# Early pairs loaded four tokens to a partition, softmax sums inverted from seven numbers, weight sides stored contiguously, and a planner with other durations

## The chip, the cores and the metric

The kernel runs on one core of a Trainium2 chip. The metric is the device time of one execution in microseconds. Besides the run times there is one profiled execution, whose trace gives every instruction of TensorE (PE; its weight loads are PEld), VectorE (DVE), ScalarE (ACT), GpSimd (POOL) and of the DMA queues (SP's, and a few on ACT and POOL).

## The reference

Attention with normalised queries and keys, then a gated feed-forward block, all in fp32 from fp64 weights:

```python
q, k, v: (8, 12, 448, 64)          # batch, heads, tokens, head size
q_n = q / sqrt(mean(q*q) + 1e-6) * g_q ;  k_n likewise
attn = softmax(q_n @ k_n.T / 8) @ v
x = attn.transpose(0, 2, 1, 3).reshape(3584, 768)
out = (silu(x @ w_gate) * (x @ w_val)) @ w_out     # 768 -> 1536 -> 768
```

The softmax needs, for each head and query, the sum of the exponentials over all keys, and the division by it.

## The kernel before, in words

**Units of work.** A *pair* is two heads of one batch; there are 48. Two batches make one *block* of the feed-forward part, so there are four blocks of twelve pairs. Pairs 0 to 11 are *early*: they run before the first block's products. The twelve pairs of a later block run beside the down products of the block before it. The matrix products are done with fifteen products of 3 x 3 sub-blocks; their left and right operands are sums and differences of sub-blocks, called *sides*. The weight sides are made once by `convert` (24 tiles: load of raw fp64 words, two ACT passes L1218 and L1222, three DVE steps for each half L1240, L1246, L1252, twelve POOL sums L1271 and L1274), stored to DRAM (`up_sides`, `down_sides`, L1299) and loaded for every block by `load_sides` (L1360) into one of two `ws` buffers.

**A pair.** `load` brings q and k. Two pairs are *natural*, four tokens to a partition (L732, one DMA a tile); the others come as 32 x 32 pieces, four DMAs a tile (L737). ACT squares them (L767), DVE sums the squares (L787 or L793), and for the pairs that are not natural the two halves of the head are exchanged by four ACT copies (L803) and added (L807). ACT and DVE form the inverse root (L682 to L690), POOL scales (L827 or L834). The operands are turned by DVE (L865; the queries then scaled on ACT, L868), or for natural pairs by PE (L853) with a drain on DVE (L859) and one on ACT (L861). Then come scores (L912), exponentials (L927), the products with v (L988), and the sums of exponentials over the keys by a product with a constant (L1019). For early pairs this last product takes all four chunks of exponentials; for the others POOL and DVE add the chunks first (L932, L938).

**The division.** The sums stand as 224 columns, repeated over 32 partitions each. DVE takes their reciprocal (L1054). For early pairs PE spreads it over the partitions by a product with the matrix `chosen` (L1062); for the others ACT does so with eight copies of 32 x 224 (L1072). ACT copies one half of the weighted sums (L1077), DVE adds the other (L1080) and multiplies (L1084).

**The feed-forward part.** `block` makes 120 up products (L1400, two matmuls each, gate and value in turn, in two banks each), whose results ACT copies (L1342) or DVE combines (L1344, L1346, L1348), then 30 down products of four matmuls each (L1574), which the next pairs' attention is laid between.

**What sets the order.** Nothing is scheduled at run time. Each piece of work is given to `Order.add` with its engine, a planned duration, a due time `when`, a rank and what it follows; `Order.run` then fills each engine's queue by the earliest planned start, ties going to the earlier due time. So the durations and the modelled DMA times fix every engine's queue, and each engine keeps to its queue in order.

```python
if piece["kb"]:
    self.dma = max(self.dma, end) + piece["kb"] / 300.0
    end = self.dma + 1.8
```

Of the kernel before, what the change touches and what calls it, by code (L numbers as in the profile page):

```python
# [359 lines left out]

class Order:
# [10 lines left out]
    SWITCH = dict(PE=0.17, ACT=1.3)  # L372

    def __init__(self, pools, begin):
        self.begin = begin
        self.pools = {name: [None] * n for name, n in pools.items()}
        self.turn = dict.fromkeys(pools, 0)
        self.users = {}
        self.pieces = []
        self.free = {}  # L380
        self.port = 0.0
        self.dma = 0.0
        self.last = {}
        self.mode = {}

    def add(
        self, engine, us, when, emit, after=(), takes=(), uses=(), port=False, kb=0, group=None,
        mode=None, early=None, rank=0.0, slack=0.1,
    ):
        piece = dict(  # L390
            engine=engine, us=us, when=when, emit=emit, takes=takes, port=port, kb=kb,
            group=group, mode=mode, early=early, rank=rank, slack=slack,
# [10 lines left out]
    def start(self, piece):  # L403
# [6 lines left out]
        for before in piece["after"]:  # L410
            if before["end"] is None:
                return None
            at = max(at, before["end"] + piece["slack"] * (before["engine"] != piece["engine"]))
        for name, _ in piece["takes"]:
            old = self.pools[name][self.turn[name] % len(self.pools[name])]
            for user in self.users.get(old, ()):
                if user["end"] is None:
                    return None
                at = max(at, user["end"] + 0.1)
        return at  # L420

    def run(self, lookahead=400):
# [3 lines left out]
        while any(left.values()):  # L426
            best = None
            for engine, pieces in left.items():
# [15 lines left out]

                late = 0.7 if engine == "POOL" else 0.0
                if choice and (
                    best is None
                    or choice[0] + late < best[0] - 0.3
                    or choice[0] + late < best[0] + 0.3
                    and self.key(choice[1]) < self.key(best[1])  # L450
                ):
                    best = (choice[0] + late, choice[1])
# [8 lines left out]
            if piece["mode"] and self.mode.get(piece["engine"]) != piece["mode"]:  # L461
                end += self.SWITCH[piece["engine"]]
                self.mode[piece["engine"]] = piece["mode"]
                if piece["mode"] in self.begin:
                    self.begin[piece["mode"]]()
            self.last[piece["engine"]] = piece
# [3 lines left out]
            if piece["kb"]:  # L470
                self.dma = max(self.dma, end) + piece["kb"] / 300.0
                end = self.dma + 1.8
# [5 lines left out]
def fast(  # L478
# [60 lines left out]
    NATURAL = (0, 1)  # L539
# [9 lines left out]
        qk=4, v=2, t=2, QT=2, KT=2, e=4, ea=7, eh=2, sums=1, inv=1, rd=1, rows=3, st=2, at=2, ss=2,  # L549
# [15 lines left out]
    OFTEN = dict(w1=0, w2=1, w3=2, w4=3, rows=4, inv=7)  # L565
# [49 lines left out]
    up_sides = [dram.tile([P, 15, 2, NC2, P], F32, name=f"up_sides{g}") for g in range(NG)]  # L615
    down_sides = dram.tile([P, 15, 2, NG, P], F32, name="down_sides")
# [13 lines left out]
    chosen = const.tile([P, 2, P], F32, name="chosen")  # L630
# [42 lines left out]
    SPREAD = 6.0  # L673

    def inverse_root(m, sums, of, when, rank=0.0):
# [9 lines left out]
        def improve():  # L685
# [7 lines left out]
            "ACT", 0.5, when, estimate, after=[sums], uses=[("ss", m)], takes=[("rr", m)],  # L693
# [3 lines left out]
            "DVE", 0.45, when + 1.0, improve, after=[first], uses=[("ss", m), ("rr", m)],  # L697
# [9 lines left out]
    def attention(m):  # L707
# [19 lines left out]
        def load(x, src):  # L727
            def emit():
# [11 lines left out]
            both = m == 0 and src is k  # L740
            queue = nc.scalar if both else nc.sync
            return add(
                "ACT" if both else "SP", 0.5 if natural else 1.4 if both else 2.4, ready - 28.0, emit, takes=[("qk", (m, x))], kb=224, early=25.0,
# [15 lines left out]
        load_v = add("SP", 2.4, ready - 16.0, load_values, takes=[("v", m)], kb=256, early=25.0)  # L759

        def square(x):
# [6 lines left out]
            if m == 0 and x:  # L768
                for _ in range(4):
                    nc.tensor.matmul(banks[0], chosen[0:R, 0], of, start=True, stop=True)  # L770

        squares = []
        for x in range(2):
            squares.append(
                add(
                    "ACT", 0.53, ready - 18.0, lambda x=x: square(x),
# [28 lines left out]
        def both():  # L805
# [6 lines left out]
            "DVE", 1.1, ready - 17.0, summed, after=squares, uses=[("t", m)], takes=[("ss", m)]  # L812
        )
        if not natural:
            sums = add("ACT", 0.9, ready - 16.0, swap, after=[sums], uses=[("ss", m)])
            sums = add("DVE", 0.15, ready - 15.0, both, after=[sums], uses=[("ss", m)])
# [6 lines left out]
        def scale(x):  # L823
            if natural:
# [16 lines left out]
                "POOL", 1.0, ready - 9.0, lambda x=x: scale(x), after=[rr], port=True,  # L841
# [32 lines left out]
        if natural:  # L874
            of_turned = ("st", (m, "turned"))
            kt, qt = [
                add(
                    "PE", 0.8, ready - 6.0, lambda x=x: turn(x), after=[scaled[1 - x]],
                    uses=[("t", m)] + [of_turned] * (1 - x), takes=[of_turned] * x, mode="full",
                )  # L880
                for x in (1, 0)
            ]
            kt = add(
                "DVE", 0.64, ready - 5.0, lambda: drain(1), after=[kt], takes=[("KT", m)],
# [3 lines left out]
                "ACT", 0.6, ready - 5.0, lambda: drain(0), after=[qt, gains], takes=[("QT", m)],  # L888
# [3 lines left out]
            "DVE", 0.62, ready - 6.0, lambda: transpose(1), after=scaled[:1], takes=[("KT", m)],  # L892
# [3 lines left out]
            "DVE", 0.62, ready - 6.0, lambda: transpose(0), after=scaled[1:],  # L896
# [3 lines left out]
            "ACT", 0.65, ready - 5.0, queries, after=[qt, gains], uses=[("qk", (m, 0))],  # L900
# [42 lines left out]
        for j in (3, 0, 1, 2):  # L943
# [4 lines left out]
                "PE", 0.41 if half else 0.76, when, lambda j=j: scores(j),  # L948
# [5 lines left out]
                "ACT", 0.5 if half else 0.92, when + 1.0, lambda j=j: exps(j),  # L954
# [3 lines left out]
            if j in (1, 2) and not early:  # L958

                def more_sums(j=j):  # L960
                    if j == 1:
# [5 lines left out]
                        "POOL", 2.15, when + 2.0, more_sums, after=[ex[j], ex[0], *adds[-1:]],  # L967
# [62 lines left out]
        for j in range(NJ):  # L1030
            half = j == NJ - 1
            last = add(
                "PE", 0.41 if half else 0.76, when + 0.01 * j, lambda j=j: weighted(j),
# [737 lines left out]
```

## Time and profile before

| | us |
|---|---|
| median of 3 runs | 1483.65 (1482.71 to 1483.81) |
| the profiled execution, its own time | 1484.42 |
| its span, first to last instruction | 1482.6 |
| first up product starts | 139.92 |
| first up products of blocks 1, 2 and 3 start | 503.9, 854.2, 1204.4 |
| last down product ends | about 1475.3 |

The page's first part gives the busy time of each engine and the number of instructions. The forty slices show the same over time, a digit being tenths of a slice. In a row of stages come the limits of the stage, its length, then busy time and number of instructions for PE, PEld, DVE, ACT and POOL, the granted TensorE clock, the busy share of the DMA engines and their GB/s. In the timeline a row is start, length, engine, line, operation, output and input, and in brackets how long the engine had stood idle and what released it. SPq and ACTq are the instructions that issue DMAs.

### The profile page before, as it was taken

What the parts mean: (1) busy time and instruction counts of PE and PEld (TensorE: products, weight loads), DVE (VectorE), ACT (ScalarE), POOL (GpSimd) and SP (SyncE); (2) the same over time, 40 slices, a digit from 0 to 9 for tenths busy, and PEclk for the clock granted to TensorE, in tenths of its full rate; (3) what the DMA queues carried; (4) which work ended last, traced back from release to release, by engine and by line L of the source; (5) the groups of instructions that cost most, each with busy time, mean ns of one, the idle gap of its engine ahead of it and who ended that gap; (6) DMA issues with size and microseconds to landing.
All of it is one profiled execution on the core that took longest, in us unless ns stands there. A gap on an engine that the chain in (4) does not pass through costs nothing.

```text
span 1482.6 us, 19482 instructions
## 1 busy us (share of the span) xinstructions
PE 1435.1 (97%) x6696; PEld 680.7 (46%) x6696; DVE 914.8 (62%) x1403; ACT 680.7 (46%) x1358; POOL 416.0 (28%) x470
## 2 busy tenths in 40 slices
PE   6989999999999999999999999999999999999998
PEld 2434554443444455544444445554444445555553
DVE  3878897877978544355886733454786753432533
ACT  5864544437775321445767422354676532122100
POOL 3545585636444100012534200011343410000000
PEclk8999999999999999999999999999999999999999
DMA  6677999974453431533344432352444442222235
GB/s 166 160 162 215 294 331 335 289 213 92 98 117 84 111 107 71 144 98 89 78 110 107 101 118 72 110 132 77 97 101 103 89 123 85 80 98 73 83 98 107
DMA packets 409457, 193.30 MB, mean 130 GB/s; under 512 B 316804, under 2 KB 391428, under 8 KB 403204
## 3 DMA queue, kind: packets, MB, share of 16 engines
q1 hardware_dynamic: 397840, 190.35, 47.8%
q10 hardware_dynamic: 11380, 1.61, 0.7%
q8 instruction: 55, 0.90, 0.3%
q14 instruction: 54, 0.44, 0.1%
q0 software_dynamic: 128, 0.00, 0.0%
HBM read 157.29 MB, written 34.60 MB: 129 GB/s over the span
## 4 chain that ended last, share of the span: by engine, by line
PE 73%; ACT 3%; DVE 3%; issue 1%; DMA 1%; SPq 1%; ACTq 0%; DVEq 0%
PE mm L1574 22%; PE mm L1400 20%; PE at L1400 20%; PE st L912 6%; PE at L988 5%; PE st L1019 1%; ACT spare L1072 1%; ACT es L927 1%; SPq L737 1%; DVE rd L1054 1%; DVE ss L807 0%; DMA work<-in_k_dram 0%; DMA out_dram<-spare 0%; DVE ss L793 0%; ACT ss L803 0%
## 5 line engine op out<-in xcount | busy, mean ns | idle before, releaser
L1400 PE MATMUL at<-xs,ws 128*128 128x448 f32 x960 | 400.6, 540 | 4.3 <-DVE v L1346 3.1
L1400 PE MATMUL mm<-xs,ws 128*128 128x448 f32 x960 | 401.0, 540 | 3.6 <-DVE spare L1348 2.2
L1400 PEld LDWEIGHTS at<-xs,ws 128*128 128x128 f32 x960 | 181.9, 190 | 184.8 <-issue 172.1
L1400 PEld LDWEIGHTS mm<-xs,ws 128*128 128x128 f32 x960 | 181.6, 190 | 184.3 <-issue 172.0
L834 POOL TENSOR_TENSOR work<-work,rr 128x448 f32<-128x448 f32 x92 | 101.8, 1126 | 480.1 <-DVE rr L690 353.3
L1574 PE MATMUL mm<-gt,ws 128*128 128x448 f32 x448 | 177.2, 545 | 0.0
L912 PE MATMUL st<-work 64*64 64x448 f32 (+1 forms) x1536 | 156.4, 514 | 18.0 <-ACT es L927 7.5
L1344 DVE TENSOR_TENSOR gt<-gt,mm 128x448 f32<-128x448 f32 x64 | 39.7, 620 | 184.2 <-PE mm L1400 181.9
L1574 PE MATMUL mm<-hs,ws 128*128 128x448 f32 x384 | 152.1, 545 | 0.9 <-DVE ss L688 0.9
L927 ACT ACTIVATE es<-st 128x896 f32<-128x896 f32 x129 | 114.1, 912 | 54.3 <-PE at L988 42.6
L932 POOL TENSOR_TENSOR sums<-es 128x896 f32<-128x896 f32 x36 | 75.8, 2104 | 196.0 <-PE st L1019 83.4
L1474 ACT ACTIVATE st<-gt 128x448 f32<-128x448 f32 x96 | 52.3, 546 | 168.9 <-DVE gt L1348 90.3
L1072 ACT COPY spare<-rd 32x224 f32<-32x224 f32 x288 | 108.1, 375 | 35.4 <-DVE rd L1054 31.1
L1574 PEld LDWEIGHTS mm<-gt,ws 128*128 128x128 f32 x448 | 82.9, 190 | 84.2 <-issue 80.6
L988 PE MATMUL at<-es,v 64*64 64x448 f32 x1032 | 109.9, 544 | 2.7 <-DVE ss L688 2.5
L1342 ACT COPY gt<-mm 128x448 f32<-128x448 f32 x80 | 42.5, 532 | 140.4 <-PE mm L1400 140.4
L1574 PEld LDWEIGHTS mm<-hs,ws 128*128 128x128 f32 x384 | 71.1, 190 | 72.9 <-issue 70.6
L912 PEld LDWEIGHTS st<-work 64*64 64x64 f32 x1536 | 50.8, 135 | 98.8 <-issue 38.1
L1342 ACT COPY v<-at 128x448 f32<-128x448 f32 x96 | 51.1, 532 | 85.1 <-PE at L1400 81.0
L932 POOL TENSOR_TENSOR sums<-sums,es 128x896 f32<-128x896 f32 x36 | 78.7, 2186 | 2.8
L865 DVE STREAM_TRANSPOSE work<-work 128x448 f32<-128x448 f32 x92 | 56.6, 627 | 25.5 <-POOL work L834 22.8
L988 PEld LDWEIGHTS at<-es,v 64*64 64x64 f32 x1032 | 39.5, 134 | 63.0 <-issue 58.7
(161 smaller groups left out, 1589.1 us busy)
## 6 DMA issues: line engine op xcount, KB each, us to landing
ws<-up_sides SPq DMA_DIRECT2D x32, 1024.0 KB, 5.0
ws<-down_sides SPq DMA_DIRECT2D x16, 1024.0 KB, 5.0
ws<-down_sides SPq DMA_DIRECT2D x28, 512.0 KB, 4.3
ws<-up_sides SPq DMA_DIRECT2D x16, 768.0 KB, 4.4
work<-in_q_dram SPq DMA_DIRECT2D x184, 56.0 KB, 2.4
work<-in_k_dram SPq DMA_DIRECT2D x184, 56.0 KB, 2.4
out_dram<-spare SPq DMA_DIRECT2D x168, 56.0 KB, 1.9
v<-in_v_dram SPq DMA_DIRECT2D x96, 96.0 KB, 2.6
```

The lines of the kernel that those rows point to most:

```text
L834: nc.gpsimd.tensor_tensor(out=tiles["t", m][:, x], in0=tiles["qk", (m, x)], in1=rr.to_broadcast([P, NC, C]), op=ALU.mult,)
L865: nc.vector.transpose(to, tiles["t", m][:, x].rearrange("p c f -> p (c f)"))
L912: nc.tensor.matmul(st[ds(D * x, D), h, 0:n], tiles["KT", m][rows, ds(P * j + D * of_keys, D)], tiles["QT", m][rows, ds(Q * of_queries, n)] ...
L927: nc.scalar.activation(e, tiles["st", (m, j)][:, :, 0 : S * width(j) // P], AF.Exp)
L932: nc.gpsimd.tensor_tensor(out=to, in0=tiles["e", (m, 0)] if j == 1 else to, in1=e, op=ALU.add)
L988: nc.tensor.matmul(tiles["at", (m, x)][ds(D * h, D), queries], tiles["v", m][rows, j, h], tiles["e", (m, j)][rows, h], start=j == 0, stop= ...
L1072: nc.scalar.copy(inv[ds(D * h + C * to, C), ts(x, Q)], tiles["rd", m][ds(D * h + C * x, C)])
L1342: nc.scalar.copy(to, ps)
L1344: nc.vector.tensor_tensor(out=to, in0=old, in1=ps, op=ALU.add)
L1400: nc.tensor.matmul(ps(), w[:, at, which, c], xs[:, SLOT[x], c], start=fresh and c == 0, stop=c == NC2 - 1, skip_group_check=True,)
L1474: nc.scalar.activation(take(*act, [P, 2, TB])[:, 0, 0:S], to, AF.Silu)
L1574: nc.tensor.matmul(banks[s][:, 0:S], w[:, at, s, g], where[x][:, g], start=fresh and g == 0, stop=g == NG - 1, skip_group_check=True,)
```

## The change

Five things change.

1. All twelve early pairs are natural: q and k come as one DMA of 224 runs of 1 KB, PE turns them, the exchange of half sums is gone for them.
2. The reciprocal. The 224 columns of sums are turned by DVE in 32 x 32 blocks, so that a partition holds seven different numbers; one reciprocal writes them twice; four ACT copies of 32 x 7 exchange them between partition groups; a second turn, with each number repeated 32 times in its input, spreads them. `chosen`, its product and the eight copies go.
3. The sides in DRAM have the fifteen sides of one tile next to each other, so a store is contiguous in each partition, while a load has four (up) or eight (down) runs in a partition.
4. The planner has other durations, a fixed delay `HOP` between engines, a model of each DMA (issue, packets, eight in flight, landing), a rank of 30 in place of 0 for the first weight tiles, and no allowance for POOL.
5. Blocks 1 to 3 start their up products in the other bank. The warm-up product follows the first square, three times in place of four.

```diff
+def transfer(rows, size):
+    return rows * (6.64 + 0.045 * min(size, 4096)) / 16000.0
...
-    SWITCH = dict(PE=0.17, ACT=1.3)
+    SWITCH = dict(PE=0.1, ACT=1.3)
+    HOP, ISSUE, LANDING, PLACES = 0.15, 0.54, 2.0, 8
...
+            for us in piece["moves"]:
+                place = self.issues % self.PLACES
+                at = max(at, self.landed[place]) + self.ISSUE
+                self.dma = max(self.dma, at - self.ISSUE + self.LANDING) + us
+                self.landed[place] = self.dma + 0.35
+                self.issues += 1
+                end = at
...
-    NATURAL = (0, 1)
+    NATURAL = (0, 1, 2, 3, 4, 5, 6, 7, 8, 9, 10, 11)
...
-    up_sides = [dram.tile([P, 15, 2, NC2, P], F32, name=f"up_sides{g}") for g in range(NG)]
-    down_sides = dram.tile([P, 15, 2, NG, P], F32, name="down_sides")
+    up_sides = [dram.tile([P, 2, NC2, 15, P], F32, name=f"up_sides{g}") for g in range(NG)]
+    down_sides = dram.tile([P, 2, NG, 15, P], F32, name="down_sides")
...
-            both = m == 0 and src is k
+            both = m == 0 and src is k and not natural
...
-            if m == 0 and x:
-                for _ in range(4):
-                    nc.tensor.matmul(banks[0], chosen[0:R, 0], of, start=True, stop=True)
+            if m == 0 and x == 0:
+                for _ in range(3):
+                    nc.tensor.matmul(banks[0], ident[0:R], of, start=True, stop=True)
...
         def invert():
-            nc.vector.reciprocal(take("rd", m, [P, Q]), tiles[den])
+            rd, rc = take("rd", m, [P, S]), take("rc", m, [P, 2, Q // C])
+            nc.vector.transpose(rd[:, 0:Q], tiles[den])
+            sums = rd[:, 0:Q].rearrange("p (one c i) -> p one c i", one=1, i=C)[:, :, :, 0]
+            nc.vector.reciprocal(rc, sums.to_broadcast([P, 2, Q // C]))
...
+        def exchange():
+            rc = tiles["rc", m]
             for h in range(2):
                 for x in range(2):
-                    for to in range(2):
-                        nc.scalar.copy(
-                            inv[ds(D * h + C * to, C), ts(x, Q)], tiles["rd", m][ds(D * h + C * x, C)]
-                        )
+                    to, of = (rc[ds(D * h + C * i, C), x] for i in (1 - x, x))
+                    nc.scalar.copy(to, of)
+
+        def spread():
+            every = tiles["rc", m].rearrange("p x (c one) -> p (x c) one", one=1)
+            nc.vector.transpose(inverse(), every.to_broadcast([P, 2 * Q // C, C]))
...
-        rank = 20.0 if by_bank else 0.0
+        rank = 20.0 if by_bank else 30.0
...
-            b = ("BCDAE".index(CHAIN[x]) % 2 if CHAIN[x] != "E" else 0) ^ (g % 2)
+            b = ("BCDAE".index(CHAIN[x]) % 2 if CHAIN[x] != "E" else 0) ^ (g % 2) ^ (n > 0)
```

## The prediction

> **What bounds the kernel now.** I read the page's busy shares and slices first, then the busy times by stage, then the timeline where TensorE stands still.
>
> ```profile
> PE 1435.1 (97%) x6696; PEld 680.7 (46%) x6696; DVE 914.8 (62%) x1403; ACT 680.7 (46%) x1358; POOL 416.0 (28%) x470
> ...
> PE   6989999999999999999999999999999999999998
> ...
> PEclk8999999999999999999999999999999999999999
> DMA  6677999974453431533344432352444442222235
> ```
>
> TensorE is the engine to watch, but "97%" hides what can be won: ends of matmuls are modelled. The loss is found from the spacing of starts.
>
> ```profile
> core 0: us, PE busy (x) PEld busy (x) DVE busy (x) ACT busy (x) POOL busy (x), PEclk, DMA share, GB/s
> ...
> 13.40:139.90 126.50, 109.86 (x1213) 49.25 (x1212) 92.60 (x157) 87.17 (x164) 56.40 (x83) 0.93 0.67 166
> 139.90:328.40 188.50, 182.78 (x486) 91.47 (x486) 155.10 (x230) 83.57 (x113) 119.03 (x228) 1.00 0.95 295
> 328.40:503.90 175.50, 169.98 (x1105) 71.65 (x1103) 139.04 (x205) 117.80 (x273) 81.27 (x48) 1.00 0.46 102
> ...
> 689.40:854.20 164.80, 162.10 (x1058) 71.75 (x1056) 124.64 (x176) 105.29 (x234) 65.01 (x38) 1.00 0.45 101
> ```
>
> Back to back, the starts of a 128-row matmul of 448 columns lie 0.752 us apart (an up product of two: 1.504); four 64x64 ones side by side also take 0.75, of 224 columns 0.375. So a pair costs at least 2.63 us for scores, 2.63 for weighted sums, 0.38 for the exponentials' sums (1.50 early, where all four chunks are summed) and 0.75 for an early pair's spread by product (L1062). Stage length less this floor:
> - early, twelve pairs: 126.5 - 90.1 = 36.4 us lost, at clock 0.93
> - block 0's up products: 188.5 - 181.2 = 7.3
> - block 0's down products with the next twelve pairs: 175.5 - (90.2 + 67.7) = 17.6
> - block 1 (503.9 to 854.2): 350.3 - 338.3 = 12.0; block 2 the same; block 3: 0.3
> - before the first stage 13.4, after the last product 7.3.
>
> A part is no stall: changing the array's shape costs, by the medians of the starts, 0.20 us (down to scores), 0.14 (sums to down), 0.12 (scores to sums), 0.05 (scores to weighted sums), some 8 to 12 us in a stage of twelve pairs. The real stalls of the early stage look like this:
>
> ```profile
> 83.28 2.21 SPq L737 DMA_DIRECT2D work<-in_k_dram  x4
> ...
> 85.45 0.58 ACT L767 ACTIVATE work<-work 128x448 f32<-128x448 f32 x1 [0.95 <-DMA work<-in_q_dram]
> ...
> 87.86 0.58 ACT L767 ACTIVATE work<-work 128x448 f32<-128x448 f32 x1 [1.84 <-DMA work<-in_k_dram]
> ...
> 88.35 0.53 ACT L927 ACTIVATE more<-st 128x448 f32<-128x448 f32 x1
> ...
> 88.92 3.27 PE L912 MATMUL st<-work 64*64 64x448 f32 x16 [3.16 <-ACT more L927]
> ```
>
> The page names ACT's exponential, but ACT was held by two squares in its queue that waited for q and k; those stood on SP behind weight loads and side stores.
>
> [...] 97% busy here with 36 us lost in one stage. [...] after the 3.16 us stall the sixteen records take 3.27 us, after no stall 1.73. [...] here a 128 B packet takes 13 ns, 512 B 28.7, 1024 B 50.8, so 128 B pays twice per byte. [...]
>
> **The change, part by part.**
>
> *Early q and k four tokens to a partition* (ten more pairs). Each tile is one DMA of 224 packets of 1 KB in place of four DMAs with 1792 of 128 B: per pair SP issues 2, not 8, at about 0.5 us each, 3 us less of SP per pair, and packet time, shared by 16 engines, falls from 2 x 1792 x 13 ns = 46.6 to 2 x 224 x 50.8 ns = 22.8 us. DVE per pair: out go two transposes (2 x 0.63), the add after the swap (0.20) and the reciprocal (1.55); in come a drain (0.62), a longer reduction (1.22 for 1.08) and one small add (0.17 or 1.03, both seen). ACT loses four swap copies (0.85) and its 0.67 scaling becomes a 0.63 drain. PE gains eight turning records at 0.096: 0.77 x 10 = 7.7 us.
>
> *Reciprocals of seven numbers.* New per pair, not in this trace: a transpose of 224 PSUM columns, [...] (bounds 0.31, half of 0.63, and 0.63); a reciprocal of 14 numbers, 0.15 to 0.25 (224 take 1.55); a transpose of 448, 0.63 by L865's row; four ACT copies 32x7, at most the 0.21 each of the 32x28 swap. [...] Early, PE loses L1062: 12 x 0.75 = 9.0 us plus its changes of shape (some 0.25 each). PE in all: -9.0 - 3 + 7.7 + 2 = -2. Late, ACT's eight copies of 0.375 become four of 0.21: 36 x 2.15 = 77 us off ACT[...]. Nearly all of it lies beside TensorE; its worth is that swaps and exponentials no longer queue behind 3 us of copies[...].
>
> *Sides contiguous.* A store is 256 packets of half 7680 B (at 159 ns per 4 KB: 2.5 us) in place of 1920 of 512 B (3.4 us); the loads split into 2 KB, 1.5 KB, 1 KB and 512 B packets. A 1.25 MB load comes to (512 x 85 + 512 x 28.7)/16 = 3.6 us against 3.1; it lands about 5 us after issue and has 15 us. Cost nil; the cover is the second ws buffer.
>
> *Planner's durations, moves and ranks* redo every queue. Reading the new order:
> - Start. All four first loads are on SP; three warm-up matmuls follow the first square instead of eight records that ended at 13.4, just before the turn. But DVE reduces pair 1 before it improves pair 0. First scores: 16.45 becomes about 14; weighted sums start about 25 instead of 31.45, since preparation no longer waits on L737. **-6 us.**
> - Rest of the early stage: 23.7 us lost now, some 9 of it shape changes; 14 are stalls and low clock at 47, 73, 85 to 95 and 118 to 126. POOL now scales five pairs before its first weight sums, so half go: **-7 us** (bounds 0 and -14). ACT needs about 91 us and DVE 86 in some 112: no bound, but less cover.
> - Up products of block 0. DVE has eight conversion halves (2.39 us apart: 19 us) between group 0's last product and group 1's first read, six now; the read is due 13.5 us on, a bank gives 4.5 more. That costs 3 to 4 us there, behind which the reads of that engine queue. The later bunches (two halves at group 2, now four) fit, and group 2's two stalls (2.1 us at 220 to 240, 1.8 at 260 to 280) should ease. SP issues group 1's first load after the store of a later tile: 0 to 2 us late. **-1 us** (bounds -5, +5).
> - Attention beside block 0's down products: seven preparation steps are now done inside the up stage; the order has as many changes of shape (about 12 us). Of 17.6 us, **-4** (0 to -6).
> - Blocks 1 and 2: the bank swap removes the wait for the last down read (0.99 less 0.11), the freed ACT the 1.84 at 766 and two of 0.4 to 0.6; the new order is regular, 8 us of changes. Of 12.0, **-4.2 each** (-2 to -4.6).
> - Last block and tail: 0.
>
> Sum: -6 - 7 - 1 - 4 - 8.4 = -26.4 us from the profiled execution's 1484.4 (span 1482.6): 1458.0. The three runs' median is 0.8 below that execution; I give **1457.5**.
>
> **Rivals.**
> - *The preparation chain stays the limit early*: squares, logarithm, scaling and turn wait for each other in order whatever the loads do. For it: DVE and ACT were only 70% busy and still PE stood. Early -5 in all, the up stage +2, the rest -9: 1471.
> - *All early stalls go*, the clock stays up, 9 us of changes remain: early -24, the rest -15: 1444.5.
> - *Slower: the turns block TensorE.* A turn now stands in PE's queue ahead of the previous pair's scores and sums, and waits for POOL, whose twelve weight sums run 6.6 us (9 x 0.5 + 3 x 0.73) without a break. Ten turns late by a mean of x cost 10x; from x = 2.9 us on the kernel is slower, at 4 us 1497. Against it: POOL has ten scalings before the first such run and stays two pairs ahead.
> - *No gain that shows*: the regrouped weight chain stalls each group of block 0 and eats the early gain: 1483.
>
> **How the numbers follow.** The sum 0.57, slow preparation 0.20, all stalls gone 0.12, no change 0.03, slower 0.08. About 0.2% (3 us) is what a measurement can tell. Faster 0.89. The range 1444 to 1478 leaves out the slow end and half of the extreme gain, and takes in the bounds of the early stage and of the up stage.
>
> **What would show it.** First up product at about 127 us (now 139.92), with no 3 us stall and the clock near 1.00; DMA share early about 0.5 for 0.67; a stall of some 3 us at the start of group 1; starts of blocks 1, 2 and 3 spaced 346 us for 350.3; L1072's 108 us replaced by about 40. Wrong: PE waiting at the turns for POOL; ws loads landing after 10 us; an early stage still above 120 us.

## The result and the profile after

The changed kernel takes **1479.7 us** (median of 8 runs, 1477.75 to 1480.93) against 1483.8 before: ratio 0.9972, interval 0.9963 to 0.998. It is faster, as forecast, but by 4 us and not by 26: the forecast was 1457.5 and its range ended at 1478. The profiled execution took 1477.75 us (span 1476.0). Between the two profiled executions lie 6.7 us; the medians differ by 2.5 us less, because the earlier profile lies 0.6 above its median and this one 1.9 below.

The page of the changed kernel, busy shares and slices:

```profile
PE 1430.8 (97%) x6726; PEld 680.8 (46%) x6726; DVE 919.6 (62%) x1484; ACT 606.8 (41%) x1222; POOL 402.3 (27%) x470
...
PEclk8999999999999999999999999999999999999999
DMA  6757999854534532543444442354445452222235
```

ACT has fallen by 74 us, about as worked out. DVE has not fallen: 919.6 for 914.8, though the first turn (0.41 us), 14 numbers (0.24) and the second turn (0.63) of a late pair together are 0.27 us shorter than the reciprocal of before (1.55). The range that follows from the prediction's bounds for these steps is 0.04 to 0.46; where in it they would lie was my estimate. That line is the first trace of where the gain went. By stages (columns as before):

```profile
core 0: us, PE busy (x) PEld busy (x) DVE busy (x) ACT busy (x) POOL busy (x), PEclk, DMA share, GB/s
11.20:131.10 119.90, 107.03 (x1249) 48.07 (x1249) 90.73 (x169) 90.15 (x169) 61.81 (x96) 0.96 0.64 190
131.10:322.20 191.10, 185.08 (x501) 92.35 (x498) 155.39 (x242) 91.80 (x133) 112.95 (x219) 0.98 0.88 286
322.20:498.90 176.70, 169.76 (x1090) 72.03 (x1089) 142.31 (x217) 90.61 (x214) 76.18 (x46) 0.99 0.47 100
684.70:849.00 164.30, 161.16 (x1058) 72.46 (x1057) 121.98 (x198) 78.89 (x186) 61.29 (x38) 1.00 0.47 100
1034.80:1197.80 163.00, 160.90 (x1058) 72.54 (x1057) 122.04 (x198) 78.85 (x186) 61.30 (x38) 1.00 0.47 101
```

The first up product starts at 131.09 for 139.92; block 0's two stages are 2.6 and 1.1 us longer than before; the attention stages of blocks 1 and 2 are 0.6 and 1.9 shorter, their up stages 0.5 longer. TensorE's waits in the changed kernel (us in total, times, longest):

```profile
PE st L926 <- ACT es L941: 8.1, 14, 3.3
PE mm L1414 <- DMA ws<-up_sides: 5.9, 1, 5.9
PE st L926 <- DVE rd L1069: 5.5, 3, 3.0
PE mm L785 <- POOL ident masks.py:199: 4.3, 1, 4.3
PE st L926 <- DVE work L874: 3.8, 2, 2.0
PE st L1033 <- ACT more L941: 2.7, 2, 1.4
```

Two are new and large behind the early stage: one load of `ws` that lands 5.9 us late, and scores (L926) that wait for DVE's first turn of the sums (L1069), because that turn frees the bank the scores write to. (L785 is the warm-up product, which waited 6.8 us for k before. L874 is DVE's drain of an operand turned by PE; its two waits lie in the early stage.) The chip's timeline shows the second:

```profile
398.73 0.37 PE L1033 MATMUL st<-sums,many 128*32 128x224 f32 x4
...
404.65 1.50 PE L926 MATMUL st<-work 64*64 64x448 f32 x16 [3.02 <-DVE rd L1069]
...
399.36 2.67 POOL L946 TENSOR_TENSOR sums<-es 128x896 f32<-128x896 f32 x1 [6.40 <-ACT v L1350]
402.11 2.12 POOL L946 TENSOR_TENSOR sums<-sums,es 128x896 f32<-128x896 f32 x1
...
400.25 1.82 DVE L702 SCALAR_TENSOR_TENSOR ss<-rr,ss 128x28 f32<-128x28 f32 x1 [0.16 <-ACT rr L697]
402.11 0.19 DVE L703 SCALAR_TENSOR_TENSOR ss<-ss,rr 128x28 f32<-128x28 f32 x1
402.33 1.94 DVE L704 SCALAR_TENSOR_TENSOR rr<-ss,rr 128x28 f32<-128x28 f32 x1
404.20 0.40 DVE L1069 STREAM_TRANSPOSE rd<-st 128x224 f32<-128x224 f32 x1
```

The sums are ready on TensorE at 399.1. In DVE's queue three operations on 28 columns stand in front of the turn. L703 takes 0.19 us, its two neighbours, of the same size, 1.82 and 1.94: each ends 0.04 us after the POOL sum beside it (402.03 and 404.23). The two take 3.4 us more than they would at L703's length, and the scores wait 3.0.

The groups of the kernel before and of the changed one (after the bar: busy time, then ns of one):

```profile
L688 DVE SCALAR_TENSOR_TENSOR ss<-rr,ss 128x28 f32<-128x28 f32 (+1 forms) x48 | 11.9, 248 | 15.4 <-ACT rr L683 15.3
L690 DVE SCALAR_TENSOR_TENSOR rr<-ss,rr 128x28 f32<-128x28 f32 (+1 forms) x48 | 10.7, 224 | 1.6
...
L702 DVE SCALAR_TENSOR_TENSOR ss<-rr,ss 128x28 f32<-128x28 f32 (+1 forms) x48 | 26.5, 552 | 14.1 <-ACT rr L697 14.0
L704 DVE SCALAR_TENSOR_TENSOR rr<-ss,rr 128x28 f32<-128x28 f32 (+1 forms) x48 | 19.2, 399 | 1.7
```

Of L702 to L704, from the first up product on, 16 of 108 last over 1 us and all take 46.9 us; in the kernel before it was 1 of 108, and 25.0 us. L822, an addition of the same size, did not grow: 2 of 36 over 1 us and 13.3 us in all, for 5 and 16.4 before. So such stretched operations are not new, but there are more of them, 19 us of DVE time in all. L702 to L704 and L822 read two inputs from SBUF each. Of these 144 operations 26 last over 0.3 us: all 26 begin while a POOL operation runs and end 0.04 to 0.05 us after it. The others take 0.19 at most; three of them run beside a POOL operation, L703 each time, and those begin within 0.002 us of its start. In the kernel before 17 of 144 last over 0.3 us, with the same two marks. Two kinds of operation in the same queue with one input are not stretched: of the 37 reciprocals L1071 after the early stage 32 begin while a POOL operation runs, and none takes over 0.243 us; L1069, which reads PSUM, does so 11 times with more than 0.04 us of it to run, and never takes over 0.42. What holds the stretched ones is not shown by the trace.

The late load stands on SP (start, length):

```profile
163.71 0.36 SPq L1305 DMA_DIRECT2D up_sides<-work  x1
164.12 3.29 SPq L1214 DMA_DIRECT2D hs<-in_moe_w_val_dram  x3
167.46 1.16 SPq L1216 DMA_DIRECT2D hs<-in_moe_w_val_dram  x2
170.26 0.33 SPq L1305 DMA_DIRECT2D up_sides<-gt  x1
170.63 3.03 SPq L1214 DMA_DIRECT2D work<-in_moe_w_gate_dram  x3
173.70 0.96 SPq L1216 DMA_DIRECT2D work<-in_moe_w_gate_dram  x2
174.75 1.20 SPq L1369 DMA_DIRECT2D ws<-up_sides  x2
```

Group 1's last tile is stored at 163.7; before its `ws` load stand two raw weight loads and a store of later groups. The load is issued at 174.75 and TensorE goes on at 182.71.

### The profile page after: what moved, and what is told of

Same layout as the page of the kernel before. It is cut to its first block, busy times and chain, and to the rows that moved or that the text cites. A ratio compares the mean times of both kernels' runs of the same rounds, so it can differ in the third digit from the quotient of the medians.

```text
span 1476.0 us, 19358 instructions
## 1 busy us (share of the span) xinstructions
PE 1430.8 (97%) x6726; PEld 680.8 (46%) x6726; DVE 919.6 (62%) x1484; ACT 606.8 (41%) x1222; POOL 402.3 (27%) x470
## 4 chain that ended last, share of the span: by engine, by line
PE 79%; DVE 4%; POOL 2%; DMA 2%; ACT 2%; issue 1%; SPq 1%; POOLq 0%; DVEq 0%; ACTq 0%
PE mm L1414 23%; PE at L1414 23%; PE mm L1592 22%; PE st L926 5%; PE at L1002 5%; PE st L1033 1%; ACT es L941 1%; DMA out_dram<-spare 1%; DVE xs L1131 1%; DMA ws<-up_sides 1%; DMA ws<-down_sides 0%; DVE sums L952 0%; DVE ss L702 0%; POOL sums L946 0%; DVE spare L1640 0%
## 5 line engine op out<-in xcount | busy, mean ns | idle before, releaser
L1414 PEld LDWEIGHTS at<-xs,ws 128*128 128x128 f32 x960 | 182.6, 190 | 180.3 <-issue 176.4
L849 POOL TENSOR_TENSOR work<-work,rr 128x448 f32<-128x448 f32 x72 | 72.8, 1031 | 449.2 <-DVE rr L704 356.4
L926 PE MATMUL st<-work 64*64 64x448 f32 (+1 forms) x1536 | 155.6, 511 | 21.0 <-ACT es L941 8.1
L1592 PEld LDWEIGHTS mm<-gt,ws 128*128 128x128 f32 x448 | 83.6, 190 | 84.8 <-issue 82.5
L926 PEld LDWEIGHTS st<-work 64*64 64x64 f32 x1536 | 49.7, 133 | 99.0 <-issue 38.8
L1352 DVE TENSOR_TENSOR v<-v,at 128x448 f32<-128x448 f32 x64 | 39.7, 620 | 41.3 <-PE at L1414 41.2
L1491 DVE SCALAR_TENSOR_TENSOR gt<-st,v 128x448 f32<-128x448 f32 x96 | 59.6, 622 | 7.5 <-DVE v L1356 0.5
```

Of the source, the lines that this page charges most:

```text
L849: nc.gpsimd.tensor_tensor(out=tiles["t", m][:, x], in0=tiles["qk", (m, x)], in1=rr.to_broadcast([P, NC, C]), op=ALU.mult,)
L926: nc.tensor.matmul(st[ds(D * x, D), h, 0:n], tiles["KT", m][rows, ds(P * j + D * of_keys, D)], tiles["QT", m][rows, ds(Q * of_queries, n)] ...
L1352: nc.vector.tensor_tensor(out=to, in0=old, in1=ps, op=ALU.add)
L1414: nc.tensor.matmul(ps(), w[:, which, c, at], xs[:, SLOT[x], c], start=fresh and c == 0, stop=c == NC2 - 1, skip_group_check=True,)
L1491: nc.vector.scalar_tensor_tensor(to, tiles[act][:, 0, 0:S], 1.0 / SCALE, tiles[ready], op0=ALU.mult, op1=ALU.mult,)
L1592: nc.tensor.matmul(banks[s][:, 0:S], w[:, s, g, at], where[x][:, g], start=fresh and g == 0, stop=g == NG - 1, skip_group_check=True,)
```

## The experiments

Each kernel was timed in five rounds beside the kernel before (1483.5 to 1484.3 in these rounds). "Early" is the start of the first up product; "block 0" runs from there to block 1's.

**Parts alone, on the kernel before.** First the banks.

```diff
-            b = (...) ^ (g % 2)
+            b = (...) ^ (g % 2) ^ (n > 0)
```

> The kernel before with one edit: the gate products of blocks 1 to 3 take the other bank at each step (the term for n > 0). Theory (parts are worth what the trace of before says, and something else gives it back): the first up product of each of blocks 1 to 3 no longer waits 0.88 us for a bank, nothing else moves, so 3 x 0.88 = 2.6 us less than before, 1481.2. Rival (the parts are worth less than the trace says): under 0.5 us, because the read that held the bank also holds the second product.

1480.2 us, ratio 0.9978 (0.9969 to 0.9987). The attention stages of blocks 1 and 2 fell from 164.89 to 164.02 each. The trace's 0.88 is confirmed to a hundredth; alone, this one term is worth nearly as much as the whole change.

This run also shows how far two executions differ. Up to 960 us every engine's instructions are those of the kernel before, in the same order, and yet the first weighted sums come at 29.78 (31.45 before) and early is 138.76 (139.92). A difference of under 2 us at the start can therefore not be put down to an edit.

```diff
+ invert, exchange, spread of the change; the product with `chosen` and the eight copies go
  (planner, layout, early pairs and banks as before; the warm-up product reads `ident`)
```

> The kernel before with the reciprocal alone: transpose, reciprocal of 14 numbers, four copies, transpose; old early pairs, old layout, old planner (but the costs of these pieces). Theory: ScalarE falls by about 74 us; the 1.84 us wait at the copies and two of about 0.5 go in blocks 1 and 2, early PE loses 12 products of 0.8 us and DVE 12 reciprocals of 1.5: 3 us less in each of blocks 1 and 2, 3 us in the early stage, about 1474.5. Rival (the longer chain of four hops on VectorE makes PE wait for VectorE in the attention stages): the S to N and L1069 waits seen after the whole change come with this part alone, and the time is 1482 or more.

1519.9 us, 36 slower. The waits of TensorE:

```profile
PE mm L1391 <- DMA ws<-up_sides: 24.4, 1, 24.4
PE at L987 <- DVE xs L1079: 17.9, 7, 5.0
```

The order that the old planner makes with this part stores the third weight tile at 166.7 us (92.2 before), so the first `ws` load is issued at 176.2; early ends at 182.2. Neither theory had that. In blocks 1 and 2 the attention stages are 163.81 and 163.92 long, 1.0 us shorter each: TensorE's wait at the copies (1.84 us by the prediction, 1.4 in the view of waits) is gone, but in block 1 that view now has 1.0 us ahead of the scores for ACT's exponentials (0.6 before) and 0.3 ahead of the sums' product.

```diff
-    NATURAL = (0, 1)
+    NATURAL = (0, 1, 2, 3, 4, 5, 6, 7, 8, 9, 10, 11)
```

> The kernel before with all twelve early pairs loaded four tokens to a partition; old layout, reciprocal and planner. Theory: nearly all of the early stage's 8.8 us comes from here (wider loads, no ScalarE swaps, no VectorE transposes; PE gets 8 transposes a pair of 0.1 us), first up product near 132 instead of 139.9, total about 1476. Rival (the early gain came from the reciprocal and the layout): first up product not under 137, total 1481 or more.

1492.2 us, 8.5 slower. Early is 137.3, 2.6 less than before and 1.5 less than in the run of the banks; then block 0's up stage takes 203.8 for 188.5.

```profile
PE mm L770 <- DMA work<-in_k_dram: 7.7, 1, 7.7
PE mm L1400 <- DVE st L1240: 7.5, 1, 7.5
```

The second line is DVE's weight conversion ahead of a read that TensorE needs.

```diff
  the changed kernel with NATURAL = (0, 1), layout, reciprocal and banks as before
```

> The planner, its measured costs and the rank of 30 alone: the changed kernel with layout, early pairs, reciprocal and banks as before. Theory A (the new order is neutral or better): 1478 to 1484. Theory B (the planner's new order is what takes the missing gain back: the weight tile of group 2 converted ahead of two of group 1 and a store and a load ahead of the ws load): the 5.9 us wait of PE for ws in block 0 is here too, and the time is 1487 or more.

1500.0 us, 16.3 slower: theory B by size, but early is 149.0, and of TensorE's 10.5 us for `ws` the longest is 6.3. The first weighted sums come at 25.0, earlier than before the change and than after it. So three of the parts alone are losses (36, 8.5 and 16 us), one is a gain of 3.3, and together they gain 4. They don't add: each is worth what the order makes of it.

**All parts, one taken out.** The old planner and costs with all other parts:

> Everything of the change but the planner: early pairs, layout, reciprocal and banks as changed; the planner's model, its costs and the conversions' rank as before. Theory A (the planner alone cost 16 us with the old parts, so without it the parts give what was forecast): 1463 or less. Theory B (parts and planner only work together: each part alone with the old costs fell behind too, 1519.9 with the reciprocal, 1492.2 with the early pairs): 1490 or more, with a wait of PE for ws or for the at bank in the early stage.

1479.9 us, the same as the changed kernel, distributed otherwise. The first weighted sums come at 21.6 us (31.45 before, 29.6 in the changed kernel), block 0 takes 356.5 us for the changed kernel's 367.8 (its attention stage 170.0 for 176.7), the attention stages of blocks 1 and 2 are 163.2 and 163.4; but early ends at 146.4, with 15.5 us of waiting for the first `ws`. SP in that kernel:

```profile
119.58 1.32 SPq L1289 DMA_DIRECT2D up_sides<-gt  x1
130.25 1.40 SPq L1198 DMA_DIRECT2D es<-in_moe_w_val_dram  x3
...
136.07 1.40 SPq L1198 DMA_DIRECT2D gt<-in_moe_w_gate_dram  x3
...
139.51 1.24 SPq L1353 DMA_DIRECT2D ws<-up_sides  x2
```

The fourth tile of group 0 is stored at 119.6, but the load of `ws` stands behind raw loads whose places come free with the last early pair only. In this order 2 of the 108 small DVE operations last over 1 us.

The sides laid out as before:

```diff
-    up_sides = [dram.tile([P, 2, NC2, 15, P], ...)]
+    up_sides = [dram.tile([P, 15, 2, NC2, P], ...)]     # down_sides, load, store and planned moves likewise
```

> The changed kernel with the sides laid out as before (a partition's run of a ws load in one piece of 4 to 8 KB; a store of 15 pieces of 512 bytes), and the planner told so. Theory (the layout is worth nothing by itself: loads 0.6 us slower, stores 1.5 us faster): within 3 us of 1479.7, apart from changes of order. Rival (the contiguous layout makes ws late in block 0): 1474 or less. Other rival (the layout is what brought the early 8.8 us): 1486 or more, first up product at 137 or later.

1482.9 us, 3.2 more than the changed kernel. `ws` is waited for 10.1 us in two waits. In block 0's up stage its 1 MB loads land 7.1 us after issue (6.5 in the changed kernel), 512 KB loads 6.9 (8.5), most stores a little later; over the whole kernel the median of the 1 MB loads of up sides is 4.9 for 5.6, about the 0.5 us that the prediction worked out. The layout is no source of the late `ws`; what of the 3.2 us is order can't be told.

The rank of the early conversions:

```diff
-        rank = 20.0 if by_bank else 30.0
+        rank = 20.0 if by_bank else 0.0
```

> The changed kernel with the early conversions' rank back at 0 (from 30), so that they no longer go ahead of the early pairs. Theory (the rank costs the ramp and pays with earlier weights): the first weighted sum comes near 22 us as with the old planner instead of 29.6, but the fourth tile is stored 10 us or more later, PE then waits 10 us or more for the first ws, and the total is 1480 to 1490. Rival (the rank is a pure loss, weights are not short): first up product at 125 or earlier, total about 1473.

1495.3 us. The wait came as in the theory,

```profile
PE mm L1414 <- DMA ws<-up_sides: 18.4, 1, 18.4
```

but the ramp did not shorten: first weighted sums at 31.5. The rank pays, and it isn't what holds the ramp. Conversely, rank 30 in the old planner:

> All parts with the old planner's model and costs, and only the early conversions' rank at 30 as changed. Theory (with the old model the parts gave a ramp 8 us shorter, block 0 7.5 us shorter and blocks 1 and 2 1.7 each, and lost 15.5 us to late weights for the first up product; the rank brings the weights ahead and gives up part of the ramp): wait for ws under 5 us, total 1466 to 1474. Rival (late weights come from the model of transfers, not from the rank): the wait stays above 10 us, total 1480 or more.

1481.4 us: wait for `ws` 8.0, between the theories; early 136.0 and the weighted sums still at 23.3, but the up stage of block 0 grew to 198.9. Another element of the planner:

```diff
+                late = 0.7 if engine == "POOL" else 0.0     # added to POOL's planned start in the choice
```

> The changed kernel with one element of the old planner back: POOL's choice counted 0.7 us later. Theory (this is what kept POOL's sums off the small VectorE operations: 1 stretched operation before, 2 with the whole old planner, 16 with the new): under 5 operations over 1 us, total 1470 to 1475. Rival (the stretch comes from the new hop, slack and durations): 10 or more over 1 us, total within 4 us of 1479.7.

1487.6 us, 10 of the 108 operations over 1 us: not this element. Which one brings the small operations beside POOL's sums was not found; it need be no single one.

**The late `ws` load.**

```diff
+        if key == ("up", 10):
+            wait = [weights["up", 7]]
```

> The changed kernel with one edit: the load of weight tile 10 (a tile of group 2, in the place hs) waits until tile 7 (the last of group 1) has been stored. Theory (the 5.9 us wait of PE for group 1's first ws comes from a tile of group 2 converted ahead of tiles 6 and 7 on ScalarE, VectorE and POOL): ws lands about 6 us earlier, the wait is gone and the time falls by 5 to 6 us to about 1474. Rival (the load is late because it is issued behind a store and a weight load on SP, or because four packets a partition land slower): the wait stays at 4 us or more and the time is within 1.5 us of 1479.7; or group 2's tiles become late in turn.

1479.6 us, and the theory is wrong. Tiles 6 and 7 are stored at 157.5 and 163.9, as in the changed kernel (157.2, 163.7): tile 10 was not in their way. Three raw loads and two stores now stand in front of `ws`, issued at 183.6; TensorE waits 14.3 us. This speaks for the place on SP.

```diff
+            if (n, g, piece) == (0, 1, 0):
+                tile_loads["up", 11]["after"].append(load)
```

> The changed kernel where the weight load of tile 11 is put after group 1's first ws load on SP (before, it was issued ahead of it, at 170.6, and the ws load at 174.8). Theory (after the hold of tile 10 changed nothing: the ws load is late because it is issued behind that load): ws issued near 170.5, the 5.9 us wait down to 1 to 2 us, total 3 to 5 us less, 1475 to 1477. Rival (tiles 6 and 7 are late by themselves, since their places are free only after the last early pair, and every us saved is given back when group 2's tiles come later): wait shorter but a new wait for a later ws; total within 1.5 us of 1479.7.

1473.5 us, but not by the theory: tile 11 lies in `es`, and the load just ahead of `ws` was that of tile 12. `ws` was issued at 176.4, the wait is 4.7. The gain lies in block 0's attention stage, 165.7 us for 176.7, where in the new order only 2 of L702 to L704 last over 1 us (8 in the changed kernel). Not all of these 11 us need be the stretch: with none at all, in the changed kernel's order, the stage takes 168.5 (below). Holding tile 12 instead (with the `port` edit below for blocks 1 and 2):

> As the one before, but tile 12's load (place work) is held behind group 1's first ws load in place of tile 11's: tile 12's was the load issued just ahead of it (170.6, ws at 174.8; holding tile 11 moved ws to 176.4). Theory (ws is late for its place on SP): ws issued near 171 to 172, PE's wait for it under 3 us of 5.9, up stage 187 to 189 us for 191.1. Rival (the store of tile 7 lands late, so ws can't go before 174): wait of 4 us or more.

1474.6 us. `ws` goes at 172.8, and the wait falls as in the theory, but another takes over:

```profile
PE mm L1415 <- DVE gt L1357: 2.9, 1, 2.9
...
PE mm L1415 <- DMA ws<-up_sides: 2.1, 1, 2.1
```

The first of these waits is new and comes two groups later, at 274.9; the second is the one for `ws`. The up stage is 189.9 for 191.1: of 5.9 us of wait 3.8 are removed and 1.2 are gained. Block 0's attention stage is 177.9, as in the changed kernel; the rest of the gain is the `port` edit's, in blocks 1 and 2 (346.6 and 347.5 us from start to start). And the first `ws` of all, in the old planner's order:

```diff
+            if (n, g, piece) == (0, 0, 0):
+                tile_loads["up", 6]["after"].append(load)
```

> All parts with the old planner, and one edit: the weight load of tile 6 (which waits for the last early pair) is put after the first ws load on SP. Theory (with the old planner the parts give all but the 15.5 us that PE waits for the first ws, issued at 139.5 behind the loads of tiles 6 to 8, though its fourth tile was stored at 119.6): ws issued near 126, first up product near 132 instead of 146.4, rest unchanged, total 1464 to 1467. Rival (tiles 6 to 8 are then late in turn and PE waits for the second or third ws in place of the first): total 1474 or more.

1474.6 us. Early 138.5; the loads of tiles 7 and 8 still stood in front (`ws` at 131.1, wait 8.7). With all three held:

> All parts with the old planner, and the loads of tiles 6, 7 and 8 put after the first ws load on SP (with tile 6 alone held, those of 7 and 8 still stood in front: ws at 131.1, PE waited 8.7 us for it). Theory (the parts are worth what was forecast once ws stands first): ws issued near 126, wait under 4 us, first up product near 133, total 1467 to 1471. Rival (tiles 6 to 8, 5 us later, make PE wait for group 1's ws): 1473 or more.

1477.9 us: early is 131.2, `ws` issued at 124.9, as in the theory; and the rival is right too, the up stage grows from 189.0 to 201.2, with 4.8 us for a later `ws` and 5.7 for two reads of DVE.

**The small operations beside POOL's sums.** Same order on every engine, POOL's sums cut short:

```diff
-                nc.gpsimd.tensor_tensor(
-                    out=to, in0=tiles["e", (m, 0)] if j == 1 else to, in1=e, op=ALU.add
-                )
+                part = (slice(None), slice(None), slice(0, 64))      # of 448 columns
+                of = tiles["e", (m, 0)] if j == 1 else to
+                nc.gpsimd.tensor_tensor(out=to[part], in0=of[part], in1=e[part], op=ALU.add)
```

> The changed kernel, same order on every engine, where POOL's two sums of a late pair (L946) add 64 of each head's 448 columns only; the rest of the sums stays at 1.0, so the denominators of the late pairs leave terms out. Theory (16 small VectorE operations last over 1 us [...] 22 us of VectorE time in all, and that makes L1069 and L952 late): no small operation over 0.6 us, VectorE's time down by about 20 us, the L1069 waits (11.5 us expected gone with their spread) vanish, block 0's attention stage falls from 176.7 to about 167, blocks 1 and 2 by about 2 each: total 1464 to 1469. Rival (the stretch hits idle time of VectorE): total within 3 us of 1479.7.

1469.5 us, 10.2 less than the changed kernel. Stages:

```profile
131.20:321.90 190.70, 185.28 (x501) 92.58 (x498) 155.30 (x242) 91.80 (x133) 112.75 (x219) 0.98 0.89 287
321.90:490.40 168.50, 167.35 (x1090) 71.60 (x1089) 121.81 (x217) 90.37 (x214) 33.65 (x46) 1.00 0.49 104
676.20:839.60 163.40, 161.10 (x1057) 72.44 (x1056) 114.71 (x198) 78.90 (x186) 25.44 (x38) 1.00 0.47 101
```

and two rows of its timeline:

```profile
398.03 0.33 DVE L708 SCALAR_TENSOR_TENSOR rr<-ss,rr 128x28 f32<-128x28 f32 x1
398.28 0.41 DVE L1073 STREAM_TRANSPOSE rd<-st 128x224 f32<-128x224 f32 x1
```

With the same instructions in the same order, block 0's attention stage is 8.2 us shorter and DVE's busy time in it falls from 142.3 to 121.8; the durations of the four small lines fall by 17.4, those of the larger sums of L1131, which also have two inputs in SBUF, by 3.1. No small operation lasts over 0.45 us (0.24 in blocks 1 and 2), and the wait for the turn is gone; these two rows are the steps that ended at 404.3 and 404.6 above. The up stage, which has no such sums, stays (190.7 for 191.1), and the wait of 5.9 there is still 5.3 (the view names a DVE step there, which ended 0.1 us before; the `ws` load is issued at 174.65). In block 1 the wait ahead of the sums' product (L1033) falls from 1.4 us to 0.4, while that of the scores for ACT's exponentials stays (1.8 and 1.9). (The two expectations that speak of waits of "5.5, 3 and 3" misread the row: 5.5 us is the total of three waits, the longest 3.0.)

The same by the order alone, nothing left out: the planner starts a piece that is marked `port` only after the marked piece before it has ended; POOL's sums have the mark, and now the small operations of late pairs get it too.

```diff
-            "DVE", 0.63, when + 1.0, improve, ...
+            "DVE", 0.63, when + 1.0, improve, ..., port=m >= EARLY,
```

(and likewise L822.)

> The changed kernel where the planner counts the small VectorE operations of the late pairs (L702 to L704, L822) as holding the port [...], so that it puts them beside no POOL sum. Theory (those operations, stretched from 0.19 to about 2 us beside POOL's sums, hold up L1069 and L952 and so cause the new waits of 5.5, 3 and 3 us in block 0 and 1.5 us in blocks 1 and 2): these waits fall to under a third, time down by 5 to 10 us. Rival (the stretch is harmless; the order on VectorE is what is late): no difference over 2 us.

1474.1 us. In blocks 1 and 2 no operation is stretched any more and the attention stages are 160.6 and 161.3 us. That is 3.6 and 1.7 less than in the changed kernel, of which the run above gives 0.9 and 1.0 to the sums; the rest is the new order itself, in which the scores of block 1 no longer wait for ACT's exponentials either. Beside block 0's down products there are still 10 of L702 to L704 over 1 us, and the stage is 175.4: there the plan no longer agrees with the chip's times. Both edits for all pairs:

> The changed kernel with the two edits that bear on different stages: small VectorE operations counted on the port (5.6 us alone), and tile 11's load after group 1's first ws load. Theory (they add): 1470 to 1472. Rival (the order moves and the gains don't add): 1474 or more.

1475.7 us, no sum: the edit of `port` changes the order of block 0's attention stage too (174.3), and the 11 us that the other edit had won there are lost. Kept apart, with `port` counted from pair 24 on:

> The changed kernel with the SP edit that kept block 0 (tile 11's load after group 1's first ws load: 1473.5, its attention stage beside block 0's down products 165.7 us for 176.7) and the port counted for the small VectorE operations of the pairs from 24 on only, which run beside blocks 1 and 2 (there it gained 3.6 and 1.7 us). Theory (the stages are separate, so the two add when the first stage's order is left alone): blocks 1 and 2 spaced 346.5 to 347 us, total 1468 to 1470. Rival (no addition, as when both were put on all pairs: 1475.7): 1473 or more.

**1467.2 us**, ratio 0.9893 (0.9876 to 0.991) to the kernel before, the fastest version. Its busy shares:

```profile
PE 1430.9 (98%) x6726; PEld 682.4 (47%) x6726; DVE 886.1 (60%) x1484; ACT 610.4 (42%) x1226; POOL 403.1 (28%) x470
```

and its stages from block 0's up products to block 2's attention stage:

```profile
133.80:328.50 194.70, 188.06 (x516) 93.00 (x513) 158.16 (x249) 102.71 (x149) 116.33 (x222) 0.98 0.90 285
328.50:494.00 165.50, 164.69 (x1073) 71.57 (x1072) 125.01 (x210) 84.97 (x202) 72.24 (x43) 1.00 0.48 102
679.90:840.50 160.60, 160.58 (x1057) 72.54 (x1056) 116.71 (x201) 78.67 (x186) 64.20 (x40) 1.00 0.48 102
1026.40:1187.80 161.40, 161.07 (x1058) 72.45 (x1057) 116.75 (x201) 78.61 (x186) 64.13 (x40) 1.00 0.47 102
```

The instruction counts of PE and DVE are those of the changed kernel, and DVE is busy 33 us less.

## Why the prediction was right and wrong

The steps, in the profiled executions (us):

| step | forecast | measured |
|---|---|---|
| start (to the first weighted sums) | -6 | -1.9 |
| rest of the early stage | -7 | -6.9 |
| up products of block 0 | -1 (-5 to +5) | +2.6 |
| attention beside block 0's down products | -4 (-6 to 0) | +1.1 |
| blocks 1 and 2 | -4.2 each (-4.6 to -2) | -0.1, -1.4 |
| last block and tail | 0 | -0.1 |
| sum | -26.4 | -6.7 |

The medians differ by 4.1 only, and the run of the banks reached its first weighted sums at 29.8 with the old order, so the 1.9 of the first row is not clear of the difference between two executions.

**The direction and the bank swap were right.** The first up product of a block no longer waits, 0.87 us per block by itself. ACT's fall and the middle of the early stage came out as worked out, and the turns did not block TensorE: POOL made them wait 1.5 us once, so the slower rival is out; the scores waited 3.8 us in two places for DVE's drain behind a turn. Of the signs that were named, L1072's 108 us became 37.4 (L1084). The early DMA share is 0.64 and not 0.5: the prediction's own packet times, ten pairs by 23.8 us on 16 engines, take 14.9 us from 84.8 us and so give an estimate of 0.62. Three sums were a little off: 120 up products of 1.504 are 180.5, not 181.2; 0.88, 1.84 and two of about 0.5 are 3.7 a block, not 4.2; and a store goes as 128 packets of 7680 B, 352 ns each on average, 2.8 us on 16 engines, not as 256 of half in 2.5.

**What failed first is "nearly all of it lies beside TensorE" for the reciprocal.** I priced DVE's operations at their short durations (0.20, 0.17) and saw the new order only as regular or not; I did not ask which of them have two SBUF inputs and would run beside POOL's sums, though the trace of before has six such over 1 us (five of L807, and L690 at 392.37: 1.95 us, to 0.04 us after a sum's end). The stretched ones put 22 us back on DVE (L702 to L704; L822 gave back 3), and since the turn of the sums is behind them in its queue, TensorE waited. With short sums and the same order, 10 us come back: 8.2 beside block 0's down products (forecast -4, measured +1.1; -7.1 without the stretch), 0.85 and 1.0 in the attention stages of blocks 1 and 2. That run shortens the sums as well as the stretch. In the timeline above the turn stands behind the stretched operations alone and not behind the sums, so the 3.0 us there are the stretch; how much of the other 7 us is due to shorter sums was not taken apart.

**Blocks 1 and 2** fell short in the term for the freed ACT as well: 1.84 and "two of 0.4 to 0.6" were read from the trace and treated as won. By itself the reciprocal brought 1.0 us a block, since other waits behind it came up, for ACT's exponentials. I had said where a stall goes, but not what is late next. With the small operations counted under `port` these waits are gone too, and the blocks follow at 346.5 and 347.2 us from start to start, where I had said 346: the gain that was forecast is there, in another order.

**Block 0's up stage**: the stall I expected for DVE's conversion halves at group 1 did not come there by itself; the 5.9 us wait was for `ws`. I had seen the load "after the store of a later tile: 0 to 2 us late", and had not counted the raw loads on SP ahead of it. Its price was right in kind and three times too small. When the load is moved up, 2.9 us for a read of DVE come to light two groups later, so little is won by mending one.

**The start**: the parts can give it, 9.8 us with the old planner; the new planner's order gave 1.9 at most. ACT's exponentials of pair 0 are queued behind a weight conversion and four squares, and the wait for them is as long as in the kernel before (3.2 us):

```profile
21.91 2.17 ACT L782 ACTIVATE work<-work 112x512 f32<-112x512 f32 x4
24.97 0.90 ACT L941 ACTIVATE es<-st 128x896 f32<-128x896 f32 x1
...
25.93 3.89 PE L926 MATMUL st<-work 64*64 64x448 f32 x24 [3.26 <-ACT es L941]
```

The new planner with the old parts starts at 25.0, so it is neither the planner nor the parts alone. The rank of the conversions is not the reason; which term of the planner it is stays open.

**"The planner's durations, moves and ranks redo every queue"** was read, but priced at nothing except where I saw a stall. Alone it cost 16 us with the old parts. With the new parts both planners come to the same time (1479.9 and 1479.7) and lose it in different places: the old one 15.5 us ahead of the first up product, the new one 8 us at the start and 11 in block 0. Each order tried leaves one queue late, the weights or the attention. The stages that are not late come near the forecast at the start (21.6, forecast 25) and beside block 0's down products (170.0, forecast 171.5), but not in blocks 1 and 2 (348.4 and 348.7 us from start to start, forecast 346). The best order found is still 9.7 us above 1457.5; its early stage ends at 133.8, where I had said 127.

## What to carry to other kernels

When every queue comes from a planner, a change of its durations is the first thing to price: run it alone with the old parts, and run the parts with the old plan, before pricing parts from one trace. For each short operation in a queue that TensorE waits for, look up in the timeline what the other engines run meanwhile, and whether it ends when one of their operations does (here 26 of 144, each 0.04 to 0.05 us after POOL's); a busy total that fails to fall with the work is the sign. Compare two executions of the same order before reading a difference of 1 or 2 us in one stage as an effect. After each repaired wait, name the next one in the same place, and expect a part of the gain only.

## What the runs showed of the hardware

- How small an operation is does not protect it: with two inputs in SBUF, on 28 columns, 0.19 us alone, it took up to 2.11 us beside a POOL sum of 896 columns (2.08 us), and at most 0.45 in the run with short sums (0.47 to 0.48 us each on average). It seems to go the other way too: the POOL sum that began at 399.36, while DVE's L1131 ran until 400.09, took 2.67 for about 2.1; it was not tested apart.
- A turn of 224 PSUM columns took 0.41 us (bounds 0.31 and 0.63), a reciprocal of 14 numbers 0.24 (0.15 to 0.25), an ACT copy of 32x7 0.195, hardly less than one of 32x28 (0.212), where one of 32x224 took 0.375: for copies this small the count sets the price more than the size.
